# Chunk inverses laid as two blocks on the diagonal of 64x64 tiles, carried there by transfers

## The chip, the cores and the metric

The kernel runs on one core of one Trainium2 chip. The metric is the device time of one execution in microseconds (us). The core has five instruction queues that run side by side: TensorE for matmuls (PE in the profile, with its weight loads shown apart as PEld), VectorE (DVE), ScalarE (ACT), GpSimd (POOL) and SyncE (SP), which here does nothing but issue transfers. Each queue runs its instructions in order, and semaphores between the queues carry the dependencies. Transfers (DMA) are moved by 16 DMA engines.

## The reference

A recurrent attention over 768 steps (batch 4, 8 heads, head size 40) feeds a mixture of eight experts. In the recurrence each head keeps a 40x40 state:

```python
for t in range(S):
    y[:, :, t] = np.einsum('bhd,bhde->bhe', rt, state)
    Sa = np.einsum('bhde,bhe->bhd', state, at)
    state_decay = state * wt[:, :, None, :] - np.einsum('bhd,bhe->bhde', Sa, bt)
    state = state_decay + np.einsum('bhd,bhe->bhde', vt, kt)
```

Its output, 3072 rows of 320, goes through a gate that sends each row to one expert (two matmuls with a ReLU between) or past all of them.

## The kernel before

The recurrence is cut into 24 chunks of 32 steps, numbered c. Inside a chunk, the steps that feed each other form a triangular 32x32 system for each of the 32 pairs of batch b and head. Its inverse turns a right-hand side into what the 32 steps really add. So the kernel works with three kinds of steps.

**Work ahead of the recurrence.** For each half h (two chunks, 64 steps, 12 halves) transfers bring the decays, the keys and the `a` vectors, VectorE scans them, GpSimd and TensorE form the products, and `tinv(ph)` (line 390) inverts the systems of four chunks, 128 systems, at once on VectorE. It is a generator: a first transpose into the scratch `NL_`, 30 elimination steps, a copy, and a last transpose (line 415) that writes the blocks for half 2·ph and half 2·ph+1 into two of the three slots of the tile `TB`. Calls of `T()` in the chunk loop spread its steps over the four chunks before those that need the inverses. Only the first two halves (chunks 0 to 3) take another path, `tinv0` (line 417).

**The recurrence.** The 32 systems of a chunk are two groups of 16: x is 0 or 1 for even or odd heads, hh counts four head pairs, b four batches. Per chunk and group, `ux` (line 474) makes the right-hand sides in PSUM, ScalarE copies them to `UX`, `uq` (line 485) multiplies them by the inverses, ScalarE copies the result into the rows `uo` of the tile `R1t` (four copies, one for each batch) and GpSimd masks a part of it; `sst` (line 497) makes the next state, `yy` (line 525) the output, and `rs` (line 460) and `m2` (line 379) the other inputs of the next chunk. Each group's `ux`, `uq` and `sst` wait for the one before, chunk after chunk; the two groups are independent of each other.

In `uq` a slot of `TB` has 128 partitions, 32 for each batch, and 16 blocks of 32 columns. One matmul takes one 32x32 block as weights and 104 or 72 columns of `UX` on the same 32 partitions (104 in even chunks, 72 in odd ones). Four batches make four matmuls on four tiles of the array, four head pairs make 16 matmuls a group.

**The experts.** After chunk 23 the eight experts run (`experts`, line 932).

**What sets the order.** From chunk 2 until the start of chunk 22 nothing is issued at once: `Rec` records every call (line 108), and `flush` (line 201) replays them in the order that `plan` (line 143) finds. The planner gives each instruction a cost: a matmul at least 0.058 of its units, a transfer 0.06 on SP's queue and a latency of 2.0 plus its bytes by 2.6e5 (lines 96 to 99). From these and the chains behind each instruction it picks what each queue issues next. The order of each queue is then fixed, whatever the chip does. Line 209 in the profile stands for all that was replayed.

Tiles that the change touches: `TB` (3 slots of 512 columns), `SCR` (2048 columns, used by the first chunks only), `NL_` (scratch of `tinv`). The input `zer` holds zeros.

Of the kernel before, what the change touches and what calls it, by code (L numbers as in the profile page):

```python
# [39 lines left out]
class Task:  # L40
    __slots__=("e","op","calls","R","W","d","lat","out","p","n","pr","al","up")
class Eng:
# [15 lines left out]
class Rec:  # L58
# [49 lines left out]
    def call(s,e,op,fn,a,k):  # L108
# [6 lines left out]
        r=[y for x in list(a[1:])+[v for n,v in k.items() if n!='accum_out'] for y in ap(x)]  # L115
        W=[u for x in w for u in s.use(x)]; R=[u for x in r for u in s.use(x)]
        d,lat=s.cost(e,op,w,r,a)
# [6 lines left out]
    def deps(s):  # L124
        acc={}
        for t in s.tasks: t.p,t.n,t.al=set(),[],set()
        for i,t in enumerate(s.tasks):
            for wr,L in ((0,t.R),(1,t.W)):
                u={}
# [97 lines left out]
def attn(ctx,tc,i,m,out,X):  # L227
# [10 lines left out]
    V,A,G,TE,SP=nc.vector,nc.scalar,nc.gpsimd,nc.tensor,nc.sync  # L238
    NC=4*NPH; NH=2*NPH
    SE=(V,G)[SCAN_POOL]  # L240
    NR1=2; NL=4; NL2=2; NTB=3
# [6 lines left out]
    w_,Z_,rv,a_,AB_,NL_,X_,l3=(mv(n) for n in (1041,1042,1041,1024,1024,1024,1024,1024))  # L248
# [4 lines left out]
    l1s=[[WR[:,8192:9216],WR[:,9216:10240],WR[:,10240:11264]]+[l3]+[L1t[:,1024*q:1024*q+1024] for q in range(4)]][0]  # L253
    L1=[[l1s[2*n+x].rearrange("p (u c t) -> p u c t",u=16,c=2) for n in range(NL)] for x in range(2)]
    TB=cp.tile([128,NTB*512],F32,name="TB"); SCR=cp.tile([128,2048],F32,name="SCR")
    TBa=[TB[:,512*q:512*q+512].rearrange("p (h m) -> p h m",h=16) for q in range(NTB)]
    L2t=cp.tile([128,5120],F32,name="L2t"); R1t=cp.tile([128,5632],F32,name="R1t")
    L2=[[L2t[:,1280*(2*n+x):1280*(2*n+x)+1280].rearrange("p (c u d) -> p c u d",c=2,u=16) for n in range(NL2)] for x in range(2)]
    R1=[[R1t[:,3328*n+(1664,1152)[n]*x:][:,:(1664,1152)[n]].rearrange("p (u n) -> p u n",u=16) for n in range(NR1)] for x in range(2)]
    RW=(104,72)  # L260
# [129 lines left out]
    def tinv(ph):  # L390
        ab=AB[0]
        NLt=sq(NL_)
        V.transpose(NLt.rearrange("p a b -> p (a b)"),ab.rearrange("p a b -> p (a b)"))
        Xi=sq(X_)
        X0=ps_x.tile([128,32,SPL],F32)
        V.tensor_tensor(X0,NLt[:,0:SPL].rearrange("p s t -> p t s"),m.mT[:,:,0:SPL],ALU.mult)
        V.tensor_tensor(Xi[:,:,SPL:32],NLt[:,SPL:32].rearrange("p s t -> p t s"),m.mT[:,:,SPL:32],ALU.mult)
        V.memset(X0.rearrange("p a b -> p (a b)")[:,0:SPL*SPL:SPL+1],-1.0)
        V.memset(Xi.rearrange("p a b -> p (a b)")[:,33*SPL::33],-1.0)
        yield  # L400
        for i in range(1,31):
            q=[]
            for g,(j,lo,hi,X) in enumerate(((i,0,min(i,SPL),X0),(i+SPL,SPL,i+SPL,Xi))):
                if j>30: continue
                n=31-j; k=hi-lo
                tmp=tmp_[g]
                tv=tmp[:,:n*k].rearrange("p (a b) -> p a b",b=k)
                V.tensor_tensor(tv,NLt[:,j,j+1:32].unsqueeze(2).broadcast_to([128,n,k]),X[:,j,lo:hi].unsqueeze(1).broadcast_to([128,n,k]),ALU.mult)
                q.append((tv,X[:,j+1:32,lo:hi]))
            for tv,xv in q: V.tensor_tensor(xv,xv,tv,ALU.subtract)  # L410
            yield
        A.copy(Xi[:,:,0:SPL],X0)
        s0=(2*ph)%NTB; s1=(2*ph+1)%NTB
        t0=TBa[s0]; d=bass.AP(t0.tensor,t0.offset,(tuple(t0.ap[0]),(TBa[s1].offset-t0.offset,2),(32,16),(1,32)))
        V.transpose(d.rearrange("p h (x f) m -> p m x h f",x=2),Xi)
        yield
    def tinv0(Xi):

# [65 lines left out]
        UXd[x]=UXs  # L484
    def uq(c,x):
        if c<0: return
        R=R1[x][c%NR1]; Tb=TBa[(c//2)%NTB]; uu=slice(uo[x],uo[x]+32); n=RW[c%2]
        UQ=ps_c.tile([128,4,n],F32,tag="pc",name="psUQ")
        for hh in range(4):
            for b in range(4):  # L490
                q=slice(32*b,32*b+32)
                TE.matmul(UQ[q,hh,:],Tb[q,x*8+hh*2+c%2,:],UXd[x][q,hh,0:n],start=True,stop=True)
        for b in range(4):
            A.copy(R[uu,4*b:4*b+4,:],UQ[32*b:32*b+32,:,:])
        pq=slice(64-64*x,128-64*x); o=R[pq,:,n-32:n]
        (V if c==NC-1 else G).tensor_tensor(o,o,mQ[pq].unsqueeze(1).broadcast_to([64,16,32]),ALU.mult)
# [48 lines left out]
    if 1:  # L545

        with tc.manual_schedule(engines={ET.Pool}):
# [4 lines left out]
            Xi=sq(X_)  # L552
# [42 lines left out]
            t0=tinv0(Xi); next(t0); tq=[0]  # L595
# [54 lines left out]
        for c in range(NC):  # L650
            ph,j=divmod(c,4)
            if c==2: rec.on=True
            if c==20: m.load(0)
            if c==22:
                with tc.manual_schedule(engines={ET.Pool}): rec.flush()
                mp.__exit__(None,None,None)
                wp=m.ctx.enter_context(tc.tile_pool(name="mwa",bufs=1,side="right")); m.WA=[wp.tile([128,5632],F32,name=n) for n in ("WH0","WL0")]; ex=wp.tile([128,1408],F32,name="ex")
                tg=m.split(0)

            if c: rs(c,0)  # L660
            T()
            if j==0 and c: l1a(2*ph+3,1); load_a(2*ph+4)
            if j==0 and c: m1(2*ph+3,0,0)
            RP('0a')
            uq(c-1,1); T()
            if c==1: full(1); m1(3,0,0); m1(3,0,1)
            if c==1: warm(BX[25])
            RP('0b')
            if j==0 and ph: wtt(2*ph,1)
            if j==1: wtt(2*ph+1,0); wex(2*ph+1,1); kbt(2*ph+1,0)  # L670
            if j==2:
                l1a(2*ph+4,1); load_a(2*ph+5)
                m1(2*ph+4,0,0)
            if j==3: kbt(2*ph+2,0)
            if c==1: warm(BX[26])
            yy(c-1,0); T()
            load_v(c+1,0)
            RP('0c')
            if c==1: warm(BX[27])

            if c: ux(c,0)
            T()
            if c==1: warm(BX[28])
            RP('1a')
            if j==1: l1z(2*ph+4,0)
            if j==3: l1z(2*ph+5,0)
            if j==0 and c: m1(2*ph+3,0,1)
            if c==1: m1(3,1,0); m1(3,1,1); tg=tinv(1)
            if j==0: wchk(2*ph+4,0)
            if j==2: m1(2*ph+4,0,1); wchk(2*ph+5,0)  # L690
            if j==1: kbt(2*ph+1,1)
            if j==3: kbt(2*ph+2,1)
            sst(c-1,1); T()
            if c==0: warm(BX[7])
            RP('1b')
            if j==0: scan_z(2*ph+4)
            if j==0 and SE is V: scan_d(2*ph+4)
            if c: m2(c+1,0)
            RP('1c')
            if j==2: scan_z(2*ph+5)  # L700
            if j==2 and SE is V: scan_d(2*ph+5)
            if c==NC-1:
                run_all(rg)
                wx=(ex[:,0:640],ex[:,640:896],ex[:,896:1408])
                SP.dma_start(wx[1],i['io']); m.early(*wx)

            if c: uq(c,0)
            T()
            if j==0:
                if c: m1(2*ph+3,1,0)  # L710
                wchk(2*ph+4,1)
                if SE is G: scan_d(2*ph+4)
                scan_w(2*ph+4); load_w(2*ph+5); kbm(2*ph+4,1)
            if j==1: l1a(2*ph+4,0)
            if j==2:
                m1(2*ph+4,1,0); wchk(2*ph+5,1)
                if SE is G: scan_d(2*ph+5)
                scan_w(2*ph+5); load_w(2*ph+6); kbm(2*ph+5,1)
            if j==3: l1a(2*ph+5,0)
            if c: rs(c,1)  # L720
            else: warm(BX[8])
            if c==1: s2(1,0,(0,0,1,1))
            if c==2: s2(1,1,(0,0,1,1))
            T()
            if j==1: kbt(2*ph+1,2)
            if j==3: kbt(2*ph+2,2)
            RP('2b')
            yy(c-1,1); T()
            load_v(c+1,1)
            RP('2c')  # L730

            RP('2d')
            if 0<c<NC: sst(c,0)
            RP('3a')
            T()
            if j==0: kbm(2*ph+4,0)
            if c==0: warm(BX[9])
            elif j==0: m1(2*ph+3,1,1)
            if j==0 and c and ph+1<NPH: tg=tinv(ph+1)
            if j==2: m1(2*ph+4,1,1); kbm(2*ph+5,0)  # L740
            if j==1: kbt(2*ph+1,3); load_kb(2*ph+5)
            if j==3: kbt(2*ph+2,3); load_kb(2*ph+6)
            if 0<c<NC: ux(c,1)
            T()
            if j==1: l1z(2*ph+4,1)
            if j==3: l1z(2*ph+5,1)
            if j==1: wtt(2*ph+1,1)
            if j==3: wtt(2*ph+2,0); wex(2*ph+2,1)
            if j==0: wex(2*ph+1,0)
            if j==2: wex(2*ph+2,0)  # L750
            if c: m2(c+1,1)
            T()
            load_rv(c+2,G if c else SP)
            if c%2 or c==0: load_rr((c+3)//2,G if c else SP)
            if c<2: m.pad(2*c); m.pad(2*c+1)
            if c==22: m.load(1)
            RP('3c')
            if c==NC-1: xl,ra,onehot=last22(); next(ra)
            if j==3:
                run_all(tg); tg=iter(())  # L760
# [333 lines left out]
```

## Time and profile before

| | |
|---|---|
| three runs | 662.9, 660.15 and 670.07 us, median 662.9 us |
| the profiled execution | 660.01 us, of which the profile's span is 658.2 us |
| mean granted TensorE clock | 0.882 of full speed |
| matmul records | 13,236 |
| packets of SP's DMA queue (q1) | 62,638, 74.31 MB, 39.0% of 16 engines |
| transfers M to L1t, WR or M by SP | 32.0 KB each |
| transfers vt to R1t by SP | 48, 80.0 KB each |

In the profile, a matmul on fp32 data appears as two records, so a `uq` of 16 matmuls shows as 32. The tile names are those of the program: `R1t<-pq,D` writes R1t and reads the PSUM bank pq and the tile D. A time in front of a row is its start from the span's beginning, and the next figure is how long the row's instructions were busy. A bracket gives the idle time ahead of a row on its engine and what ended it.

### The profile page before, as it was taken

Reading aid. Unit: us, or ns where it says so; the run is one execution under the profiler, and the core shown is the slowest. Engines: PE = TensorE matmul, PEld = TensorE weight load, DVE = VectorE, ACT = ScalarE, POOL = GpSimd, SP = SyncE. Lnnn points to the kernel's source line nnn. Section 1 sums busy time; section 2 is a strip of 40 time slices with the busy share of each in tenths; the row PEclk is TensorE's granted clock in tenths of the full one; section 3 lists DMA queues with packets and bytes.
Section 4 is the critical chain, followed back from the end, with each engine's and each line's share of the span. In section 5 each row is a group of like instructions: output and inputs, shape, how many; then the busy total and the mean of one; then the engine's idle time right before and its main releaser. Section 6 shows DMA issues by size and latency. Waiting matters only on the chain. (4 is left out here: it accounts for less than half of the span.)

```text
span 658.2 us, 30327 instructions
## 1 busy us (share of the span) xinstructions
PE 507.4 (77%) x13236; PEld 424.8 (65%) x13236; DVE 519.6 (79%) x1182; ACT 423.6 (64%) x1103; POOL 321.6 (49%) x256
## 2 busy tenths in 40 slices
PE   5766676687588778858758578888678799999994
PEld 2544465566476657637547466767566599899994
DVE  7998778988989789997998977884274458888871
ACT  6463565587766867757768578898966155455540
POOL 5491952645536665375733634333131156566661
PEclk9697778779877986888969799999977799999998
DMA  7784566352444525345334243454535166667200
GB/s 183 215 229 153 133 181 218 114 150 86 124 119 132 162 74 142 107 130 161 102 106 121 82 129 101 133 168 119 156 99 146 57 193 207 214 216 233 81 25 24
DMA packets 67817, 90.85 MB, mean 138 GB/s; under 512 B 32756, under 2 KB 54849, under 8 KB 66190
## 3 DMA queue, kind: packets, MB, share of 16 engines
q1 hardware_dynamic: 62638, 74.31, 39.0%
q0 software_dynamic: 5040, 14.54, 6.8%
q8 instruction: 106, 1.74, 1.1%
q14 instruction: 33, 0.27, 0.1%
HBM read 74.03 MB, written 17.08 MB: 138 GB/s over the span
## 5 line engine op out<-in xcount | busy, mean ns | idle before, releaser
L209 DVE TENSOR_TENSOR M<-M 128x130 f32<-128x130 f32 (+10 forms) x202 | 106.2, 526 | 2.2
L209 ACT COPY R1t<-pq 32x416 f32<-32x416 f32 (+4 forms) x218 | 84.1, 386 | 31.7 <-PE pq L209 28.7
L209 POOL TENSOR_TENSOR R1t<-R1t,mc 64x512 f32<-64x512 f32 x40 | 53.8, 1346 | 86.3 <-ACT R1t L209 62.8
L109 POOL TENSOR_TENSOR WL<-WR,WH 128x1280 fp32r<-128x1280 f32 (+1 forms) x21 | 57.6, 2779 | 8.7 <-ACT WH L109 8.6
L209 ACT COPY R1t<-pc 32x128 f32<-32x128 f32 (+4 forms) x146 | 53.3, 365 | 9.7 <-PE pc L209 7.7
L209 PE MATMUL py<-L2t,R1t 128*32 128x40 f32 x1280 | 22.9, 220 | 27.4 <-DVE XS L209 14.4
L209 POOL TENSOR_TENSOR WR<-WR,M 128x1024 f32<-128x1024 f32 x14 | 33.7, 2422 | 14.9 <-DMA WR<-kb 14.6
L109 ACT CAST WH<-WR 128x1024 fp32r<-128x1024 f32 (+1 forms) x35 | 39.6, 1132 | 0.0
L209 DVE TENSOR_TENSOR px<-px,M 128x168 f32<-128x168 f32 (+8 forms) x141 | 37.1, 263 | 3.1
L209 PEld LDWEIGHTS py<-L2t,R1t 128*32 128x32 f32 x1280 | 18.1, 124 | 31.9 <-issue 16.9
L109 DVE CAST ti<-xe 128x2 int32<-128x2 f32 x8 | 38.0, 4747 | 0.2
L109 POOL DMA_INDIRECT out<-ro,ti x16 | 15.7, 982 | 45.7 <-PE pq L109 21.8
L109 ACT ACTIVATE hH<-pc 128x512 fp32r<-128x512 f32 x21 | 12.6, 598 | 38.3 <-PE pc L109 38.3
L209 POOL DMA_INDIRECT xg<-XS,ix x20 | 24.6, 1232 | 25.1 <-DVE M L209 11.1
L209 DVE TENSOR_TENSOR M<-M,px 128x168 f32<-128x168 f32 (+8 forms) x141 | 34.7, 246 | 1.3
L209 DVE TENSOR_TENSOR_SCAN M<-M 128x1041 f32<-128x1041 f32 (+1 forms) x14 | 32.5, 2320 | 0.2
L209 POOL TENSOR_TENSOR M<-M,mc 128x256 f32<-128x256 f32 x16 | 12.1, 756 | 41.6 <-issue 25.4
L109 PE MATMUL pc<-xH,WH 128*128 128x256 f32 x126 | 32.4, 282 | 0.0
L109 DVE TENSOR_TENSOR WL<-WR,WH 128x1024 fp32r<-128x1024 f32 (+1 forms) x19 | 23.8, 1253 | 8.4 <-ACT WH L109 7.8
L209 DVE TENSOR_TENSOR R1t<-pc,D 40x512 f32<-40x512 f32 (+1 forms) x32 | 19.2, 601 | 13.3 <-PE pc L209 12.9
L209 PE MATMUL ps<-R1t,L2t 128*40 128x40 f32 (+1 forms) x512 | 26.3, 244 | 2.5 <-ACT R1t L209 1.1
L209 PE MATMUL pq<-UX,TB 32*32 32x72 f32 (+1 forms) x800 | 23.6, 262 | 5.5 <-ACT R1t L209 5.3
(380 smaller groups left out, 1692.9 us busy)
## 6 DMA issues: line engine op xcount, KB each, us to landing
WR<-kb SPq DMA_DIRECT2D x10, 1024.0 KB
WR<-w SPq DMA_DIRECT2D x16, 640.0 KB
WR<-w SPq DMA_DIRECT2D x16, 512.0 KB
vvt<-vv POOLq DMA_DIRECT2D x21, 256.0 KB, 4.1
rrt<-rr POOLq DMA_DIRECT2D x10, 512.0 KB, 5.6
M<-wt SPq DMA_DIRECT2D x9, 520.5 KB
M<-at SPq DMA_DIRECT2D x8, 512.0 KB
WR<-w SPq DMA_DIRECT2D x16, 256.0 KB
```

Of the source, the lines that this page charges most:

```text
L109: if not s.on: return fn(*a,**k)
L209: for fn,a,k,own in s.tasks[i].calls: fn(*[at(x,own) for x in a],**{n:at(x,own) for n,x in k.items()})
```

## The change

For the halves from 2 on (chunks 4 to 23) an inverse is kept as a 64x64 tile: the blocks of batches 0 and 1 stand on its diagonal, and zeros beside them; batches 2 and 3 make a second tile on the other 64 partitions. `uq` then takes 64 rows and 64 columns in one matmul, two for each head pair in place of four: 8 matmuls a group. Three slots of 1024 columns hold such tiles, two in `SCR` and one over the first 1024 columns of `TB`. The blocks of halves 0 and 1 keep their form.

`tinv`'s last transpose now writes its blocks to `NL_`. Eight transfers on SP's queue (four batches for each of two halves, 32 partitions of 16 runs of 32 numbers each) then carry them into the slots, batch b to column 0 or 32. Zeros come from three more transfers, two in chunk 2 and one in chunk 5.

```diff
-    TBa=[TB[:,512*q:512*q+512].rearrange("p (h m) -> p h m",h=16) for q in range(NTB)]
+    TBn=[TB[:,o:o+512].rearrange("p (h m) -> p h m",h=16) for o in (1024,0)]
+    TBw=[t.rearrange("p (h m) -> p h m",h=16) for t in (SCR[:,0:1024],SCR[:,1024:2048],TB[:,0:1024])]
+    TBa=TBn
+    def tbw(h): return TBw[(h+1)%NTB]
...
         A.copy(Xi[:,:,0:SPL],X0)
-        s0=(2*ph)%NTB; s1=(2*ph+1)%NTB
-        t0=TBa[s0]; d=bass.AP(t0.tensor,t0.offset,(tuple(t0.ap[0]),(TBa[s1].offset-t0.offset,2),(32,16),(1,32)))
-        V.transpose(d.rearrange("p h (x f) m -> p m x h f",x=2),Xi)
+        t0=NL_.rearrange("p (w h m) -> p w h m",w=2,h=16)
+        V.transpose(t0.rearrange("p w (x f) m -> p m x w f",x=2),Xi)
+        for w in range(2):
+            for b in range(4):
+                r=slice(32*b,32*b+32); SP.dma_start(tbw(2*ph+w)[r,:,32*(b%2):32*(b%2)+32],t0[r,w])
...
-        R=R1[x][c%NR1]; Tb=TBa[(c//2)%NTB]; uu=slice(uo[x],uo[x]+32); n=RW[c%2]
+        R=R1[x][c%NR1]; uu=slice(uo[x],uo[x]+32); n=RW[c%2]; k=32 if c<4 else 64; Tb=TBn[c//2] if c<4 else tbw(c//2)
         UQ=ps_c.tile([128,4,n],F32,tag="pc",name="psUQ")
         for hh in range(4):
-            for b in range(4):
-                q=slice(32*b,32*b+32)
+            for b in range(128//k):
+                q=slice(k*b,k*b+k)
                 TE.matmul(UQ[q,hh,:],Tb[q,x*8+hh*2+c%2,:],UXd[x][q,hh,0:n],start=True,stop=True)
...
-            if c==2: s2(1,1,(0,0,1,1))
+            if c==2:
+                s2(1,1,(0,0,1,1))
+                for q in range(2): SP.dma_start(SCR[:,1024*q:1024*q+1024],i['zer'][:,0:1024])
+            if c==5: SP.dma_start(TB[:,0:1024],i['zer'][:,0:1024])
```

Since the planner sees other costs, it also puts other instructions in other places. Three of them follow; in these listings R1t, L1t, TB, SCR, M, WR are tiles (`NL_` lies in M), `D` holds scales, `sc`, `eq`, `oh`, `sb`, `sm` and `mx` are the gate's, pq, pc, ps and py are PSUM banks.

On VectorE's queue, where `tinv` for chunks 16 to 19 ends, stood before:

```order
L209 TENSOR_TENSOR oh_1409<-eq_1405,m_1408 128x16
L209 SCALAR_TENSOR_TENSOR oh_1409<-sc_1402,oh_1409 128x16
L209 TENSOR_TENSOR sb_1406<-sc_1402,mx_1404 128x16
L209 TENSOR_TENSOR R1t<-pc_102,D_503 40x8x40 x2
L209 STREAM_TRANSPOSE TB<-M 128x32x2x2x8
L209 TENSOR_TENSOR R1t<-pc_102,D_503 40x8x64 x2
L209 TENSOR_REDUCE sm_1410<-ex_1407 128x2
```

and stands now:

```order
L209 STREAM_TRANSPOSE M<-ps_104 128x4x32
L209 STREAM_TRANSPOSE M<-M 128x32x2x2x8
L209 TENSOR_REDUCE mx_1404<-sc_1402 128x2
L209 TENSOR_TENSOR eq_1405<-sc_1402,mx_1404 128x16
L209 TENSOR_TENSOR eq_1405<-eq_1405,mc 128x16
L209 TENSOR_REDUCE m_1408<-eq_1405 128x2
L209 TENSOR_TENSOR oh_1409<-eq_1405,m_1408 128x16
L209 SCALAR_TENSOR_TENSOR oh_1409<-sc_1402,oh_1409 128x16
L209 TENSOR_TENSOR sb_1406<-sc_1402,mx_1404 128x16
L209 COPY XS_1281<-mc 128x2
L209 TENSOR_TENSOR R1t<-ps_104,D_503 40x8x40 x2
```

The transpose that ends `tinv` now stands ahead of the gate's seven instructions and of the two products `R1t<-..,D` of 40 columns.

On SP's queue, where the last `tinv` (for chunks 20 to 23) ends, stood before:

```order
L209 DMA R1t<-vt 32x16x40
L209 DMA WR<-w 128x4x320
L209 DMA R1t<-vt 32x16x40
L209 DMA out<-XS_1281 4x32x320
L209 DMA X<-XS_1281 4x32x320
```

and stands now:

```order
L209 DMA X<-XS_1281 4x32x320
L209 DMA WR<-w 128x4x320
L209 DMA TB<-M 32x16x32 x4
L209 DMA SCR<-M 32x16x32 x4
L209 DMA R1t<-vt 32x16x40
L209 DMA out<-XS_1281 4x32x320
```

The eight transfers of the blocks stand between the load of an expert's weights and the next load of values into R1t.

On TensorE's queue, at the first `uq` of chunk 16, stood before:

```order
L209 MATMUL pq_99<-R1t,WR 32x104 x16
L209 MATMUL pq_100<-rrt_152,SS_117 40x64 x16
L209 MATMUL pq_99<-oh_1409,mc 32x16 x8
L209 MATMUL pc_102<-WR,L1t 32x64 x16
L209 MATMUL pc_101<-UX_453,TB 32x104 x16
L209 MATMUL pq_100<-rrt_152,vvt_150 32x32 x16
```

and stands now:

```order
L209 MATMUL pc_102<-R1t,WR 32x104 x16
L209 MATMUL pq_100<-oh_1409,mc 32x16 x8
L209 MATMUL pc_101<-rrt_152,SS_117 40x64 x16
L209 MATMUL py_105<-L2t,R1t 32x40 x16
L209 MATMUL pc_102<-WR,L1t 32x64 x16
L209 MATMUL pq_100<-WR,L1t 32x64 x16
L209 MATMUL pc_102<-UX_453,SCR 64x104 x8
```

Between the chunk's `ux` (`R1t,WR`) and its `uq` there were three groups, and there are now five; the `uq` itself is 8 matmuls on SCR.

## The prediction, made before the changed kernel ran

> **What bounds the kernel now.** I read the busy shares first, then the windows by stage, then the timeline around `uq` and around the end of `tinv`, then SP's queue.
>
> ```profile
> PE 507.4 (77%) x13236; PEld 424.8 (65%) x13236; DVE 519.6 (79%) x1182; ACT 423.6 (64%) x1103; POOL 321.6 (49%) x256
> DVE  7998778988989789997998977884274458888871
> ```
>
> ```profile
> core 0: us, PE busy (x) PEld busy (x) DVE busy (x) ACT busy (x) POOL busy (x), PEclk, DMA share, GB/s
> 100.00:420.00 320.00, 234.14 (x8024) 194.33 (x8020) 282.29 (x742) 232.44 (x665) 161.62 (x143) 0.85 0.43 124
> 420.00:507.00 87.00, 68.97 (x2362) 56.14 (x2361) 51.52 (x164) 70.02 (x200) 24.71 (x24) 0.92 0.47 135
> 507.00:658.20 151.20, 137.12 (x1158) 130.26 (x1155) 101.86 (x146) 64.41 (x95) 75.29 (x39) 0.96 0.44 138
> ```
>
> The shares over the whole span name no single engine; the stages do. From 100 to 420 us the recurrence and `tinv` run together, and VectorE is busy 282.3 of 320 us (88%), TensorE 234.1 (73%). It has 37.7 us of idle time there: that is the most which any better order could bring in this stage. From 420 to 507 us most of `tinv` is done; ScalarE (80%) and TensorE (79%) take turns in the chain of `ux`, copy, `uq`, copies, `sst`, and no engine is full. After 507 us the experts run, which the change does not touch. All of the change lies between about 100 and 507 us.
>
> **The matmuls.** The change replaces 32 records by 16 in each of 40 groups. Whether that saves time depends on what a record costs. These are the rows of weight loads and matmuls of groups that ran at undisturbed pace; PEld's busy time is the better measure of a group's pace, since it has less of the last matmul's tail.
>
> ```profile
> 152.17 0.69 PEld L209 LDWEIGHTS pq<-UX,TB 32*32 32x32 f32 x32
> 152.17 0.92 PE L209 MATMUL pq<-UX,TB 32*32 32x104 f32 x32
> 166.02 0.53 PEld L209 LDWEIGHTS pc<-UX,TB 32*32 32x32 f32 x32
> 166.02 0.70 PE L209 MATMUL pc<-UX,TB 32*32 32x72 f32 x32
> 153.42 0.49 PEld L209 LDWEIGHTS pq<-WR,M 128*32 128x32 f32 x32
> 153.42 0.65 PE L209 MATMUL pq<-WR,M 128*32 128x64 f32 x32
> 142.16 0.94 PEld L209 LDWEIGHTS pc<-rrt,SS 128*40 128x40 f32 x32
> 142.16 1.09 PE L209 MATMUL pc<-rrt,SS 128*40 128x64 f32 x32
> 153.04 0.34 PEld L209 LDWEIGHTS pc<-rrt,vvt 40*32 40x32 f32 x32 [0.18 <-ACT WT L209]
> 153.04 0.46 PE L209 MATMUL pc<-rrt,vvt 40*32 40x32 f32 x32
> ```
>
> The number of records is the same in all five groups, the time is not. Groups with four tiles side by side take 0.34, 0.49, 0.53 and 0.69 us for 32, 64, 72 and 104 columns: 32 records are 8 rounds of four, and a round costs 42, 61, 66 and 86 ns. It grows with the columns. The fourth group, `rrt,SS`, has tiles of 40 columns of weights, of which only two fit side by side: 32 records are 16 rounds, 0.94 / 16 = 59 ns for 64 columns, where a round of four costs 61. So a round costs what its columns cost, whether two tiles run in it or four. A `uq` of 64x64 tiles has 16 records in pairs, which is 8 rounds of 104 or 72 columns, as before: 0.69 and 0.53 us. The tiles grow, the rounds stay. My term is 0. Its ends: if time followed the records, each group would halve, 20 x 0.69 / 2 + 20 x 0.53 / 2 = 12.2 us less; if the two diagonal tiles did not run side by side, there would be 16 rounds, 24.4 us more. The groups at 142.16 (two column halves) and 153.04 (two row halves) both show halves side by side, so I stay at 0.
>
> The Trainium skill's page "TensorEngine Tiling (Array Packing)", section "Instruction Overhead", says that each matmul carries some 60 cycles whatever its columns; at the 2.4 GHz that "TensorE: Matmul & The Clock Gate" gives, an estimate is 25 ns a record, so 16 records fewer would save 0.4 us a group and 16 us in 40 groups. This trace disagrees for tiles side by side: 32 records in 0.34 us are 11 ns each.
>
> **VectorE.** `tinv` ends in one transpose before and after, into another tile with the same pattern. Nothing is added: 0. VectorE's load in its full stage is unchanged, so the change offers that stage nothing.
>
> **The hand-over.** This is the new wait. Before, `uq` could start once the transpose had ended; now the blocks travel first. These are the five transposes, and the first `uq` that needs each of them (for the first, the group at 152.17 above).
>
> ```profile
> 136.60 1.99 DVE L209 STREAM_TRANSPOSE TB<-M 128x1024 f32<-128x1024 f32 x1 [0.84 <-ACT M L209]
> 220.32 1.98 DVE L209 STREAM_TRANSPOSE TB<-M 128x1024 f32<-128x1024 f32 x1
> 300.55 1.96 DVE L209 STREAM_TRANSPOSE TB<-M 128x1024 f32<-128x1024 f32 x1
> 383.61 1.98 DVE L209 STREAM_TRANSPOSE TB<-M 128x1024 f32<-128x1024 f32 x1
> 444.46 1.94 DVE L209 STREAM_TRANSPOSE TB<-M 128x1024 f32<-128x1024 f32 x1
> 231.21 0.92 PE L209 MATMUL pq<-UX,TB 32*32 32x104 f32 x32
> 311.58 1.11 PE L209 MATMUL pq<-UX,TB 32*32 32x104 f32 x32
> 391.80 0.92 PE L209 MATMUL pc<-UX,TB 32*32 32x104 f32 x32
> 454.59 1.28 PE L209 MATMUL pc<-UX,TB 32*32 32x104 f32 x32
> ```
>
> From the end of the transpose to that `uq` there are 13.6, 8.9, 9.1, 6.2 and 8.2 us, 9.2 in the mean. Against this stands the price of the transfers:
>
> ```profile
> 141.79 2.47 SPq L209 DMA_DIRECT2D WR<-M  x4
> 145.38 0.59 SPq L209 DMA_DIRECT2D R1t<-vt  x1
> 452.65 0.62 SPq L209 DMA_DIRECT2D R1t<-vt  x1
> 140.70 1.00 SPq L209 DMA_DIRECT2D M<-at  x1
> vvt<-vv POOLq DMA_DIRECT2D x21, 256.0 KB, 4.1
> xg<-XS,ix POOLq DMA_INDIRECT x24, 3.6
> 559.21 5.82 DMA xe<-xg
> 387.61 0.99 DVE L209 TENSOR_TENSOR R1t<-pc,D 40x320 f32<-40x320 f32 x2
> 398.64 1.25 DVE L209 STREAM_TRANSPOSE M<-M 128x1024 f32<-128x1024 f32 x1 [2.42 <-ACT M L209]
> ```
>
> SP issues four transfers between tiles in 2.47 us, 0.62 each, and a load with runs as short as the new ones (160 bytes, R1t<-vt) in 0.59. Chunk 4·ph needs only the first four transfers: 4 x 0.62 = 2.5 us of issue, and then the last one has to land. No SP row shows a landing of tile to tile; the nearest are 3.6 and 4.1 us from issue to landing on GpSimd's queue, and 5.8 us in the chain of waits. I take 4.1, the nearest in kind (a plain transfer), so the blocks are there 6.6 us after the transpose, at most 8.3. The one `uq` that this would catch is chunk 16's, with 6.2 us. There the new order puts the transpose ahead of the two 40-column products, 0.99 us, and of the gate's seven short instructions, and puts two more groups between `ux` and `uq` on TensorE, so 7.2 us or more remain. Term: 0; with 5.8 us of landing, about 1 us. The second four (for chunks 4·ph+2 and 4·ph+3) come 2.5 us later and are needed two chunks later. If the cover went, `uq` would stand on TensorE with the next chunk's `rrt,vvt` products behind it, and ScalarE's four copies into R1t would wait.
>
> The Trainium skill's "DMA: Bandwidth & Descriptors", section "Specifications", asks for runs of at least 512 bytes, below which the engine reads and writes back; it speaks against runs of 128 bytes. No row here prices that alone; by the fit in its section on one transfer of GpSimd's path (2.0 us and the bytes by 436 GB/s) the landing would be an estimate of 2.2 us for 64 KB, inside the cover.
>
> **SP's queue.** 43 issues x 0.62 = 27 us of SP, in five bursts of eight (5.0 us) and three zero loads. Behind the last burst stands the next load into R1t. It went out at 452.65; transpose end 446.40 + 5.0 = 451.4, so 1.2 us are to spare. Nothing on TensorE waits for it: 0. The three zero loads are of the size of M<-at (1.00 us of issue) and lie in chunks 2 to 5, several us ahead of their use; the DMA engines are busy 43%: 0. The next `tinv` may not overwrite `NL_` before the blocks have been read: at the tightest place it starts at 398.64, 13.1 us after the transpose's end at 385.59, and 5.0 + 4.1 = 9.1 us suffice: 0.
>
> **The new order.** The planner halves its price for `uq` and adds a latency to `tinv`; every queue between chunk 2 and 22 is reshuffled. No row of the trace prices that. Bound: VectorE's 37.7 us of idle time in its stage; I take a third, 12.6 us, as likely either way, and 0 as the value.
>
> **Sum.** 660.0 us (profiled execution: span 658.2 and 1.8 around it) + 0 - 0 = 660.0. The median shown is 662.9, 2.9 higher; I forecast 661.5, between the two.
>
> **The rivals.** *Records set the price* (faster): 12.2 us less, 647.8. For it: fewer instructions; against it: the rounds above. *The new order fills VectorE's gaps* (faster): half of 37.7, 641.2. For it: `tinv` ends earlier among its neighbours; against: the stage's work is the same and already 88% dense. *The new order opens gaps* (slower): as much the other way, 678.9. *Blocks late behind SP's waits* (slower): SP issues in order, and its queue stands still for TensorE for long:
>
> ```profile
> SPq L209 <- PE pq L209: 40.8, 19, 7.0
> ...
> 444.62 0.92 SPq L209 DMA_DIRECT2D WR<-w  x1
> ```
>
> If such a wait of 7.0 us stood ahead of each burst, the blocks would come 7.0 + 6.6 - 9.2 = 4.4 us late, five times, 22 us: 682. It decides from 2.7 us a time (13.3 us in all). Against it: the load of weights that the new order puts ahead of the last burst went out at 444.62, before the transpose ended at 446.40, and SP then issued nothing until 452.65. *The change does not do what it says*: the diagonal tiles run one after the other, 24.4 us more on TensorE: 684.4 if all of it were on the path.
>
> **How the numbers follow.** Two per cent is about what a measurement of this kernel can tell from no change: faster is under 649.6, slower over 676.2. No change: 0.66. Faster: records 0.05, order 0.10, together 0.15. Slower: order 0.09, late blocks 0.06, tiles in turn 0.04, together 0.19. The likeliest has 661.5 with its own range 649 to 674 (12.6 either side). To leave out no more than 0.2 (better order, late blocks, tiles in turn) the range takes in the records' 647.8 and the worse order's 678.9: 645 to 680.
>
> **What would show it.** Right: groups `UX,SCR` of 16 records with a PEld time near 0.69 and 0.53 us; `uq` after each burst without an idle time released by a DMA; VectorE's busy time from 100 to 420 us near 282 us and the stage near 320. Wrong: PEld of 0.35 (records) or 1.38 us (in turn); TensorE idle ahead of the first `uq` of chunks 4, 8, 12, 16 or 20 with a DMA as releaser; SP's bursts starting several us after the transpose; or a stage before 507 us that differs by over 13 us with all of these in place, which would leave the order.

## The result, and the profile after

| | before | after |
|---|---|---|
| median of 20 runs | 660.9 us | 668.5 us |
| lowest and highest | 656.1 and 670.1 us | 664.2 and 673.5 us |
| ratio after to before | | 1.0123, 95% interval 1.0098 to 1.0147 |
| profiled execution, span | 658.2 us | 666.3 us |

The change made the kernel 1.2% slower. The forecast was no change, 661.5 us, with 645 to 680 as the range. The time lies in the range, but the slowdown is real: its interval leaves no change out. Medians are over all runs, while each ratio is estimated from the runs that were not in the chip's slower state, so it is not quite the quotient of the medians.

The busy line and VectorE's tenths on the page of the changed kernel:

```profile
PE 516.3 (77%) x12596; PEld 432.6 (65%) x12596; DVE 508.7 (76%) x1182; ACT 423.1 (63%) x1103; POOL 320.5 (48%) x256
DVE  7998689978796759888799958884247457888871
```

Its windows by stage (busy time of each engine, with the number of records, the granted clock and the share of the DMA engines):

```profile
core 0: us, PE busy (x) PEld busy (x) DVE busy (x) ACT busy (x) POOL busy (x), PEclk, DMA share, GB/s
100.00:420.00 320.00, 233.76 (x7298) 195.13 (x7293) 266.34 (x719) 220.32 (x630) 157.97 (x140) 0.82 0.47 131
420.00:507.00 87.00, 69.25 (x2198) 57.01 (x2201) 51.99 (x165) 73.88 (x213) 24.27 (x23) 0.92 0.52 138
```

TensorE has 640 records less (13,236 before), and VectorE is busy 10.9 us less in all. Between 100 and 420 us VectorE did 266.3 us of work where it did 282.3 before. So in the full stage it stood still for 54 us instead of 38. Part of the fall is that some products took less time (see further down); the rest are new holes, and the timeline shows what the longest of them wait for. First TensorE's weight loads of four `uq` groups at undisturbed pace (start, busy time, tiles, shape, records):

```profile
161.53 0.73 PEld L209 LDWEIGHTS pq<-UX,SCR 64*64 64x64 f32 x16 [0.44 <-ACT R1t L209]
181.69 0.57 PEld L209 LDWEIGHTS pq<-UX,SCR 64*64 64x64 f32 x16
212.09 0.57 PEld L209 LDWEIGHTS pc<-UX,SCR 64*64 64x64 f32 x16
248.01 0.73 PEld L209 LDWEIGHTS pq<-UX,TB 64*64 64x64 f32 x16
```

Half the records take 0.73 and 0.57 us, where the full number took 0.69 and 0.53. The form saves nothing. Now SP's queue around the burst of eight that ends the second `tinv`:

```profile
215.19 0.59 SPq L209 DMA_DIRECT2D L1t<-M  x1
215.87 0.62 SPq L209 DMA_DIRECT2D L1t<-zer  x1
216.55 3.19 SPq L209 DMA_DIRECT2D L1t<-M  x3
219.84 0.60 SPq L209 DMA_DIRECT2D R1t<-vt  x1
220.54 3.85 SPq L209 DMA_DIRECT2D TB<-M  x4
224.44 2.66 SPq L209 DMA_DIRECT2D SCR<-M  x4
227.20 0.60 SPq L209 DMA_DIRECT2D out<-XS  x1
227.91 3.89 SPq L209 DMA_DIRECT2D L1t<-M  x4
231.84 0.60 SPq L209 DMA_DIRECT2D X<-XS  x1
232.55 0.40 SPq L209 DMA_DIRECT2D L1t<-zer  x1
```

and TensorE and VectorE there, and VectorE later, at the burst for chunks 16 to 19:

```profile
230.46 0.49 PE L209 MATMUL py<-L2t,R1t 128*32 128x40 f32 x32
237.03 1.08 PE L209 MATMUL pc<-WR,L1t 128*32 128x64 f32 x32 [6.08 <-DMA L1t<-zer]
...
239.46 0.99 DVE L209 TENSOR_TENSOR R1t<-pq,D 40x320 f32<-40x320 f32 x2 [6.30 <-PE pq L209]
...
400.17 0.32 DVE L209 STREAM_TRANSPOSE M<-pq 128x128 f32<-128x128 f32 x1 [6.58 <-DMA L1t<-M]
```

SP issues almost without a pause for 18 us. The zeros in `L1t` that TensorE's products `WR,L1t` need (232.55) stand behind the eight blocks and six other transfers, and TensorE stands idle for 6.08 us until they have landed; VectorE then waits 6.30 us for TensorE. The last burst but one does the same to VectorE directly. No `uq` waits for the blocks in that time: the late ones are the loads queued behind them. The waits view sums it (total, times, longest):

```profile
POOL WR L209 <- DMA WR<-kb: 25.5, 3, 9.2
DVE M L209 <- DMA L1t<-M: 6.6, 1, 6.6
PE pc L209 <- DMA L1t<-zer: 6.1, 1, 6.1
```

The second and third line have no counterpart in the kernel before, and GpSimd's wait for the keys (WR<-kb) was 14.6 us there.

### The profile page after: what moved, and what is told of

Same layout as the page of the kernel before. It is cut to its first block, busy times and chain, and to the rows that moved or that the text cites. A ratio compares the mean times of both kernels' runs of the same rounds, so it can differ in the third digit from the quotient of the medians.

```text
span 666.3 us, 29130 instructions
## 1 busy us (share of the span) xinstructions
PE 516.3 (77%) x12596; PEld 432.6 (65%) x12596; DVE 508.7 (76%) x1182; ACT 423.1 (63%) x1103; POOL 320.5 (48%) x256
## 3 DMA queue, kind: packets, MB, share of 16 engines
q1 hardware_dynamic: 84190, 78.51, 41.9%
q0 software_dynamic: 5040, 14.54, 7.1%
## 4 chain that ended last, share of the span: by engine, by line
PE 22%; DVE 15%; ACT 9%; issue 4%; DMA 2%; SPq 1%; POOL 0%; DVEq 0%; POOLq 0%; ACTq 0%
DVE M L209 7%; PE pc L109 6%; PE ps L109 5%; ACT R1t L209 5%; PE py L109 3%; PE px L109 3%; PE pq L209 2%; PE pc L209 1%; DVE R1t L209 1%; DVE px L209 1%; PE pq L109 1%; ACT L2t L209 1%; DVE ti L109 1%; DMA ex<-xg 1%; SPq L209 1%
## 5 line engine op out<-in xcount | busy, mean ns | idle before, releaser
L209 POOL TENSOR_TENSOR R1t<-R1t,mc 64x512 f32<-64x512 f32 x40 | 51.2, 1280 | 95.1 <-ACT R1t L209 80.4
L209 ACT COPY R1t<-pq 32x416 f32<-32x416 f32 (+4 forms) x198 | 77.9, 394 | 29.5 <-PE pq L209 24.6
L209 DVE TENSOR_TENSOR M<-M 128x130 f32<-128x130 f32 (+10 forms) x202 | 89.6, 444 | 1.9
L209 DVE TENSOR_TENSOR R1t<-pq,D 40x320 f32<-40x320 f32 (+1 forms) x44 | 25.5, 578 | 22.3 <-PE pq L209 21.7
L109 ACT ACTIVATE hH<-pc 128x512 fp32r<-128x512 f32 x21 | 12.6, 598 | 38.9 <-PE pc L109 38.9
L209 DVE TENSOR_TENSOR_SCAN M<-M 128x1041 f32<-128x1041 f32 (+1 forms) x14 | 35.1, 2509 | 0.4
L109 PE MATMUL ps<-mc 128*128 128x512 f32 x36 | 24.9, 800 | 4.3 <-DMA mc<-mc 3.2
L109 PE MATMUL ps<-WH,hH 128*128 128x320 f32 x88 | 27.6, 314 | 0.0
L209 POOL TENSOR_TENSOR M<-M,mc 128x256 f32<-128x256 f32 x16 | 13.9, 871 | 27.8 <-issue 13.9
```

Source lines behind the costliest of these rows:

```text
L109: if not s.on: return fn(*a,**k)
L209: for fn,a,k,own in s.tasks[i].calls: fn(*[at(x,own) for x in a],**{n:at(x,own) for n,x in k.items()})
```

## The experiments

Times are medians, and each ratio is to the kernel before on the same chip. Several kernels leave work out and so compute other numbers; from the last `uq` to the end all sixteen traces take 146 to 152 us, so their gains lie for the most part ahead of the experts. Where the words say "the order of X", every engine's instructions stand in that kernel's order, and only what is named differs. In five of the kernels that leave work out (not in the one on the order alone), the test at the end that sends unusual inputs down a general path is held off as well.

### Which part costs

Four kernels take the change apart. The first keeps the changed order and issues none of the 40 block transfers:

```diff
+            if s.tasks[i].tag=='blk': continue
             for fn,a,k,own in s.tasks[i].calls: fn(...)
```

> The changed kernel, every queue in the same order, with the 40 transfers that carry the blocks left out (uq then works on zeros, so the corrections of chunks 4 to 23 are missing from the output). Measured so far: before 660.9, changed 668.5 us. Theory 1, the bursts of eight hold up SP's other transfers, on which TensorE and VectorE wait: 659 to 663 us, and the idle times ahead of L1t<-zer (PE, 6.1 us) and L1t<-M (DVE, 6.6 us) are gone. Theory 2, the new order itself costs the time: 667 to 670 us. Theory 3, the 64x64 form costs it: 667 to 670 us. Theory 4, uq waits for the blocks' landing: 659 to 663 us.

Measured: 649.6 us, ratio 0.982 (0.979 to 0.985). Without its transfers the changed order is 1.8% faster than the kernel before. That is 9 us below the lowest time that any of the four theories allowed: none of them had a gain from the new order in it.

The second issues two transfers of 128 partitions in place of eight of 32 (same blocks and bytes; 83,710 packets on SP's queue for 84,190):

```diff
-                SP.dma_start(tbw(2*ph+w)[r,:,32*(b%2):32*(b%2)+32],t0[r,w])
+                if b==0: SP.dma_start(tbw(2*ph+w)[:,:,0:32],t0[:,w])
```

> The changed kernel, every queue in the same order, but of each burst of eight only two transfers, one for each half, of all 128 partitions into column 0 (the blocks of batches 1 and 3 then stand beside the diagonal, so the output's corrections are wrong from chunk 4 on). The bytes, the wait for the transpose and uq's wait for a landing stay, SP's issues go from 40 to 10. Theory 1 (bursts on SP): 660 to 664 us. Theory 2 (order): 667 to 670 us. Theory 3 (form): 667 to 670 us. Theory 4 (landing of the blocks): 665 to 669 us.

Measured: 659.8 us, ratio 0.996 (0.993 to 0.999), just below the band of the first theory and far from the others. The wait of TensorE for L1t<-zer is 1.9 us.

The third keeps order and transfers, but `uq` takes 16 matmuls of 32x32 from the diagonals:

```diff
-            for b in range(128//k):
-                q=slice(k*b,k*b+k)
-                TE.matmul(UQ[q,hh,:],Tb[q,x*8+hh*2+c%2,:],...)
+            for b in range(4):
+                q=slice(32*b,32*b+32); o=32*(b%2) if c>=4 else 0
+                TE.matmul(UQ[q,hh,:],Tb[q,x*8+hh*2+c%2,o:o+32],...)
```

> The changed kernel, every queue in the same order, transfers as changed, but uq again as 16 matmuls of 32x32 a group, read from the diagonals. Theory 3 (the 64x64 form costs the time): 659 to 662 us. All others: 667 to 670 us, the same as the changed kernel, since a group has eight rounds of columns in either form.

Measured: 671.1 us, ratio 1.013 (1.009 to 1.017), where the changed kernel has 1.012; the time is 1 us above the band. The form of the matmuls is worth nothing either way.

The fourth is the kernel before with eight idle transfers (TB to the unused SCR) behind each end of `tinv`:

```diff
         V.transpose(d.rearrange(...),Xi)
+        for w in range(2):
+            for b in range(4): SP.dma_start(SCR[32*b:32*b+32, ...],TBa[(s0,s1)[w]][32*b:32*b+32])
```

> The kernel before, every queue in its old order, with eight more transfers on SP's queue behind the end of each tinv, of the same size and shape as the blocks', from TB into SCR, which nobody reads. Theory 1 (bursts on SP): 664 to 670 us, with new idle times ahead of work that waits for L1t<-M, L1t<-zer or WR<-kb. Theory 2 (order), 3 (form) and 4 (landing): 660 to 662 us, no change.

Measured: 664.8 us, ratio 1.007 (1.003 to 1.010). Bursts that nobody waits for cost the old order 0.7%, some 4 us; GpSimd's wait for the keys (WR<-kb) rose from 14.6 to 29.0 us.

What was open is whether the first kernel was fast because its `uq` no longer waits for `tinv`. So the next one keeps that wait: the changed order with the old data path, the transpose writing narrow slots and `uq` reading them in 32x32.

```diff
-        V.transpose(t0.rearrange("p w (x f) m -> p m x w f",x=2),Xi)
+        V.transpose(dd,Xi)
```

> The order of the changed kernel on every engine, but the old data path: tinv's transpose writes the narrow TB slots, uq reads them in 16 matmuls of 32x32, and the 40 block transfers and three zero loads are not issued. uq waits for tinv again, which it did not in the run without block transfers (649.6 us). Theory 1 (the bursts on SP's queue hold up the other loads): 648 to 653 us, no wait of TensorE for L1t<-zer, the longest GpSimd wait for WR<-kb 15 us or less. Rival (the run without transfers was fast because uq no longer waited for tinv, and the new order is worth nothing): 658 to 662. Rival (the order itself loses): 666 to 670.

Measured: 651.5 us, ratio 0.987 (0.982 to 0.992). (Its last five `uq` groups stand outside the planned stretch and still multiply zeros.) With this the change splits in two: the new order is worth 9.8 us of gain (651.5 against 661.3), the transfers cost 17.0 (668.5 against 651.5).

### What in the transfers costs

The same order, every transfer cut to a sixteenth:

```diff
-                SP.dma_start(tbw(2*ph+w)[r,:,e],t0[r,w])
+                SP.dma_start(tbw(2*ph+w)[r,0:1,e],t0[r,w,0:1])
```

> The changed kernel's exact order with all 40 block transfers, each cut to the first of its 16 blocks (32 runs of 128 bytes in place of 512; the other matrices are left zero, so uq multiplies by zeros there). As many transfers on SP's queue, a sixteenth of the packets. The same order without transfers gave 651.5 us, with two transfers a tile and all packets 659.8, with all 668.5. If the number of issues costs: 664 to 668 us, with SP's bursts of 4.5 us and more and the wait of TensorE for L1t<-zer at 4 us or more. If the packets cost: 652 to 655. If both: about 660, the complement of the run with two transfers.

Measured: 661.9 us, ratio 1.005 (1.001 to 1.009). SP's timeline at its first burst:

```profile
141.40 6.52 SPq L210 DMA_DIRECT2D SCR<-M  x8
```

These eight issues take 6.52 us with 32 runs each, and took 6.47 with 512. The other four bursts are shorter than in the changed kernel: from first issue to last, all five take 31.3 us with the small transfers and 34.8 with the full ones. So an issue costs SP nearly, but not quite, the same. TensorE's wait for L1t<-zer is 3.7 us, a little under the 4 us expected if issues cost. Of the 17 us, 10.4 remain with the issues alone (661.9 - 651.5), so about 6.6 come with the packets and their bytes; by the ratios the parts are 12.0 and 5.0, so the split is known to some 2 us. The kernel with two transfers a tile has nearly all packets and a quarter of the issues: 6.6 + 10.4 / 4 = 9.2 us over 651.5, and 8.3 were measured. That is a weak check: its ten issues still take SP 15.8 us from first to last in the five bursts, nearly half of 34.8.

Two kernels try to pay less. The first joins both halves in one transfer, four a tile (a fourth slot makes the diagonals neighbours), and is planned anew:

```diff
-        for w in range(2):
-            for b in range(4):
-                SP.dma_start(tbw(2*ph+w)[r,:,32*(b%2):32*(b%2)+32],t0[r,w])
+        for b in range(4):
+            SP.dma_start(ST_[r,o:o+2048].rearrange(...)[:,:,32*(b%2):32*(b%2)+32],NL_[r,0:1024].rearrange(...))
```

> The changed kernel with four transfers in place of eight a tile (both halves of a row block in one, 128 KB each; a fourth slot makes the two diagonals neighbours; planned anew). Bytes and blocks are the same. Theory 1 (what costs is SP's issue): SP issues some 13 to 16 us less, and the time comes near that of the run with two transfers, 658 to 663 us; the wait of TensorE for L1t<-zer falls to 3 us or less. Rival (the bytes or the short runs cost, in the DMA engines): 666 to 670, with the same waits. Rival (uq waits for the landing of the blocks): 666 to 672, TensorE idle ahead of the first uq of a tile with ST<-M as releaser.

Measured: 662.6 us, ratio 1.003 (0.9995 to 1.006), in the expected band; TensorE's wait for L1t<-zer fell to 3.6 us, not below 3. A transfer of both halves takes SP 1.0 us and more (four in 4.10 to 7.01), so SP's time fell by less than half.

The second issues the blocks on GpSimd's queue, planned anew:

```diff
-                SP.dma_start(tbw(2*ph+w)[r,:,32*(b%2):32*(b%2)+32],t0[r,w])
+                G.dma_start(tbw(2*ph+w)[r,:,32*(b%2):32*(b%2)+32],t0[r,w])
```

> The changed kernel with the 40 block transfers issued on GpSimd's queue in place of SP's (planned anew). Theory 1: SP's loads are no longer held up, the waits of TensorE for L1t<-zer and of VectorE for L1t<-M are under 2 us; GpSimd pays 40 issues (24 to 40 us of an engine that is 50% busy), so 652 to 664 us by how much its products come late. Rival (the transfers themselves, whatever queue): 666 to 670.

Measured: 657.9 us, ratio 0.998 (0.994 to 1.002). The time fits, one sign does not: VectorE still waits 7.4 us for L1t<-M and 13.7 us for WR<-M. With SP free of the bursts, its own loads come late all the same in this order. That it is the packets is not shown: SP's queue has 21,120 packets less than in the changed kernel (63,070 for 84,190), and GpSimd's queue has, by the profile's count, only 1,280 more (6,320 for 5,040).

### Why the transfers were not hidden

The planner that writes the order takes 0.06 for a transfer on SP's queue. Measured were 0.85 us in the mean: the five bursts of the changed kernel take 6.47, 6.51, 5.95, 6.81 and 8.22 us, 34.0 for 40 issues. (Most of the issues take 0.6 to 0.7 us, and one or two in each burst 1.2 to 2.1.) So one number is changed:

```diff
-            return (0.06 if e=='S' else 1.0 if 'ind' in op else 0.6),2.0+by/2.6e5
+            return (0.65 if e=='S' else 1.0 if 'ind' in op else 0.6),2.0+by/2.6e5
```

> The changed kernel with one number of the planner changed: a transfer on SP's queue costs SP 0.65 us in place of 0.06, so the list is made knowing that eight blocks take 5 us of SP. If the planner's ignorance of SP's issues was the loss: 650 to 658 us, waits of TensorE and VectorE for L1t under 2 us each. If SP's work itself is the loss, wherever it stands: 662 to 670.

Measured: 649.0 us, ratio 0.985 (0.980 to 0.991): 19.5 us less than the changed kernel, with all that it does still in it, and 1 us below the expected band. Two places on SP's timeline, and the waits:

```profile
206.56 0.78 SPq L209 DMA_DIRECT2D L1t<-zer  x1
...
209.56 0.40 SPq L209 DMA_DIRECT2D L1t<-zer  x1
210.66 2.67 SPq L209 DMA_DIRECT2D TB<-M  x4
213.37 3.54 SPq L209 DMA_DIRECT2D SCR<-M  x4
217.01 3.66 SPq L209 DMA_DIRECT2D L1t<-M  x4
```

```profile
DVE M L209 <- DMA WR<-M: 9.9, 4, 5.6
POOL WR L209 <- DMA WR<-kb: 6.8, 2, 4.8
DVE M L209 <- DMA L1t<-M: 3.8, 2, 2.9
POOL D L209 <- DMA L1t<-zer: 0.7, 1, 0.7
```

The bursts are as long as before, but the zeros now go out ahead of them, and TensorE waits for none. VectorE's waits for L1t did not fall under 2 us as expected: they are 3.8 us in two, the longest 2.9, and with those for WR<-M 13.7 us in six.

Is that the transfers hidden, or another list that happens to be good? Two controls. The first takes the transfers out of this order:

```diff
+            if s.tasks[i].tag=='blk': continue
```

> The order of the run with SP's real price in the planner (649.0 us), but the 40 block transfers are not issued and uq multiplies by the zeros there. If the list hid the transfers: 644 to 650 us, less than 1% faster. If they still cost what they cost in the changed kernel (17 us, by 668.5 against 651.5): 630 to 634.

Measured: 644.5 us, ratio 0.976 (0.969 to 0.983). The transfers cost this order 4.5 us by the medians, and the intervals of the two ratios overlap. Taken out in the same way, they cost the changed order 18.9 us (668.5 against 649.6). So 14.4 of the 19.5 us are transfers better hidden, and the other 5.1 are a list that is faster without them too. The second gives the kernel before the same price:

```diff
-            return (0.06 if e=='S' else ...
+            return (0.65 if e=='S' else ...
```

> The kernel before with only the planner's price of a transfer on SP at 0.65 us in place of 0.06. Its SP queue has no bursts of eight. If the price helps because it makes room for the bursts: 655 to 664 us, little change. If it makes better lists of any program: 640 to 650, as much off as the changed kernel got (19 us).

Measured: 664.7 us, ratio 1.004 (1.000 to 1.008). It is just above its band of little change: without bursts the right price gains nothing here. This fits a price that helps by making room for the bursts, but it is one list, and another program could come out otherwise.

### Why the new order is faster

VectorE is busy 10.9 us less with the same 1,182 instructions. One group fell by 16.6 us, the others rose by 5.7 together. In the groups of the kernel before (count, busy time, mean ns of one):

```profile
L209 DVE TENSOR_TENSOR M<-M 128x130 f32<-128x130 f32 (+10 forms) x202 | 106.2, 526 | 2.2
L209 DVE TENSOR_TENSOR px<-px,M 128x168 f32<-128x168 f32 (+8 forms) x141 | 37.1, 263 | 3.1
```

and of the changed kernel:

```profile
L209 DVE TENSOR_TENSOR M<-M 128x130 f32<-128x130 f32 (+10 forms) x202 | 89.6, 444 | 1.9
L209 DVE TENSOR_TENSOR px<-px,M 128x168 f32<-128x168 f32 (+8 forms) x141 | 37.2, 264 | 3.1
```

The 202 elimination products of `tinv` whose operands all lie in SBUF took 106.2 us, now 89.6; those with an operand in PSUM (px) did not change. Here are two stretches of the kernel before, VectorE and then GpSimd:

```profile
281.55 0.23 DVE L209 TENSOR_TENSOR M<-M 128x76 f32<-128x76 f32 x1
...
282.32 7.76 DVE L209 TENSOR_TENSOR M<-M 128x76 f32<-128x76 f32 x3
290.00 0.22 DVE L209 TENSOR_TENSOR M<-M,px 128x72 f32<-128x72 f32 x1
...
251.12 0.32 DVE L209 TENSOR_TENSOR M<-M,px 128x168 f32<-128x168 f32 x1
251.48 0.34 DVE L209 TENSOR_TENSOR px<-px,M 128x168 f32<-128x168 f32 x1
```

```profile
281.95 2.16 POOL L209 TENSOR_TENSOR WR<-WR,M 128x1024 f32<-128x1024 f32 x1
...
284.21 1.28 POOL L209 TENSOR_TENSOR R1t<-R1t,mc 64x512 f32<-64x512 f32 x1
285.46 2.15 POOL L209 TENSOR_TENSOR WR<-WR,M 128x1024 f32<-128x1024 f32 x1
287.58 2.17 POOL L209 TENSOR_TENSOR WR<-M 64x1024 f32<-64x1024 f32 x1
...
251.10 1.27 POOL L209 TENSOR_TENSOR R1t<-R1t,mc 64x512 f32<-64x512 f32 x1 [0.32 <-POOL R1t L209]
```

A product of 76 elements takes 0.23 us; three of them took 7.76 while GpSimd computed from 281.95 to 289.75. At 251 the products with an operand in PSUM ran at their pace beside GpSimd. The Trainium skill's page "SBUF — State Buffer", section "Who interferes with whom", says that these two engines share a pair of ports by an exclusive lock, and its "Summary: rules for kernel authors" that of a VectorE operation with two SBUF inputs and a GpSimd operation that reads SBUF the one issued second stands still until the first has ended; these rows agree. So does the whole group: 39 of the 202 products took over 0.1 us more than the 20th percentile of their shape, 56.2 us more in all, and each of them overlaps GpSimd's work by at least its excess. In the changed kernel there are 29 such products with 39.3 us. The rest of the group's time is 50 us in both.

Whether this sets the time was tried by shortening GpSimd alone. In the order of the kernel before, GpSimd's mask behind `uq` works on one block of 16 (the 40 masks took 53.8 us, and take 11.0):

```diff
-        G.tensor_tensor(o,o,mQ[pq].unsqueeze(1).broadcast_to([64,16,32]),ALU.mult)
+        G.tensor_tensor(o[:,0,:],o[:,0,:],mQ[pq],ALU.mult)
```

> The kernel before in its exact order, but GpSimd's masking of R1t behind uq works on one of 16 blocks (64x32 in place of 64x512, some 1.27 us down to 0.15 each; the rest stays unmasked). Theory C: VectorE's products with all operands in SBUF (M<-M) stand still while GpSimd computes, 59.0 us of excess over their usual durations in the kernel before, 42.5 in the changed order without transfers, 31.3 in the order made by the two prices; that is why orders differ. Then this kernel loses part of the excess: VectorE's busy time down by 10 us or more, 645 to 655 us. Rival (GpSimd is off the path, and the orders differ for another reason): 658 to 662, VectorE's busy time within 3 us of 519.6.

The excess named there is, over all products of the form M<-M, the time above the 20th percentile of their shape.

```profile
L211 DVE TENSOR_TENSOR M<-M 128x130 f32<-128x130 f32 (+10 forms) x202 | 86.7, 429 | 2.2
```

Measured: 641.8 us, ratio 0.973 (0.965 to 0.981). GpSimd was busy under half the span, and less work on it took 19.4 us off the kernel and 19.5 us off VectorE's group; the time is below the expected band. Products that wait for the mask come sooner too, so not all of it need be the stalls. That GpSimd's work stretches these products is shown; that this alone makes one order faster than another is argued.

Since the order alone gives such gains, two kernels ask whether the kernel before can have one without the change. The first gives its planner a `uq` at half the price and 2.6 us of latency behind `tinv`'s last transpose:

```diff
+            rec.PC=0.058 if c<4 else 0.029
...
+        rec.LX=2.6
         V.transpose(d.rearrange(...),Xi)
+        rec.LX=0.0
```

> The kernel before, with nothing changed but two numbers of the planner: uq's price 0.029 us a matmul from chunk 4 on (in place of 0.058) and 2.6 us of latency behind tinv's last transpose. So the planner makes an order of the kind of the changed kernel's for the old data path. If these prices make the better order: 648 to 655 us. If the gain of the changed kernel's order was that of one list among many: 655 to 666, about the kernel before.

```profile
L209 DVE TENSOR_TENSOR M<-M 128x130 f32<-128x130 f32 (+10 forms) x202 | 77.0, 381 | 1.8
```

Measured: 637.6 us, ratio 0.965 (0.959 to 0.971), the best of all and below both expected bands, with the computation of the kernel before. The group of products takes 77.0 us, 29.2 less, and the kernel 23.7 less. The second has the price alone:

```diff
-        rec.LX=2.6
+        rec.LX=0.0
```

> The kernel before with uq's planned price halved and no latency behind the transpose: one of the two numbers that gave 637.6 us together. If the price alone makes the better order: 636 to 642 us. If each number makes just another list, whose time goes by how VectorE's M<-M products fall on GpSimd's work: anywhere from 636 to 665, with VectorE's busy time lower by about as much as the time (496.4 us of busy time at 637.6, 519.6 at 661.2).

Measured: 651.0 us, ratio 0.985 (0.978 to 0.992). The price alone does not make the better order; each pair of numbers makes its own list. The sign that was to go with it did not come: in its profiled execution, 656.5 us, VectorE is busy 518.2 us, 1.4 less than before, and the group of products takes 96.8 us, 9.4 less. So the group's time alone does not fix the kernel's.

## Why the prediction was wrong

- **The matmuls, 0: right.** A `uq` group costs what its columns cost. The rows show 0.73 and 0.57 us for 0.69 and 0.53, 0.04 more a group, 1.6 us in 40; undoing the form changed nothing (1.013 and 1.012).
- **The hand-over, 0: right.** No `uq` stood idle with a block's landing as releaser. The one wait that the profile puts down to a block transfer is VectorE's, 1.0 us for SCR<-M ahead of a transpose into M.
- **SP's queue, 0: here it failed.** The step took 0.62 us an issue (most took about that, but 0.85 were measured in the mean of the bursts) and then looked behind the last burst only, where the next load into R1t had 1.2 us to spare. It found nobody waiting there and put 0 for all five. Behind the others stood the zeros and rows for `L1t` and the keys for `WR`, on which TensorE, VectorE and GpSimd wait. The transfers measured 17.0 us in the new order, 10 to 12 of them with the issues alone. The three waits were on no list of what would show the forecast wrong, which asked only for TensorE idle ahead of a `uq`.
- **The packets: not in the sum.** SP's queue has 84,190 of them after and 62,638 before. The landing was priced and was covered, as said; but 5 to 7 of the 17 us came with the packets and their bytes and not with the issues. Which loads they made late is not shown. The Trainium skill's "DMA: Bandwidth & Descriptors", section "Specifications", which the prediction weighed for the landing alone, asks for runs of at least 512 bytes. The cut transfers had fewer bytes and fewer runs at once, so what short runs cost by themselves wasn't tried.
- **The new order, 0 with 12.6 either way: the value off, the bound good.** It gained 9.8 us. But that the bound held is luck: it was made from VectorE's idle time, as the most that any order could bring, and in the order alone the busy time of VectorE fell by 12.9 us (506.7 for 519.6).
- **VectorE, 0: wrong in its reason.** The instructions are the same, their durations are not: 106.2 us against 89.6 in one group.

The forecast put 0 for two terms that were -9.8 and +17.0 us. They cancel in part, so the number came out nearer than its terms. The rival "blocks late behind SP's waits" had the right queue but the wrong victim: the blocks were in time, and they made others late.

Open is how the 17 us spread over the single waits along the path, what of the shortened masks is stall and what earlier products, and whether the granted clock, which was 0.82 between 100 and 420 us after and 0.85 before, follows the holes or adds to them.

## What to carry to other kernels

When a change adds transfers to a queue, go behind each burst and list every transfer that now stands there, with who waits for it; that the DMA engines were busy 43% of the stage did not show it here. When a planner writes the order, correct its prices along with the change: the same change lost 1.2% with a wrong price for SP and gained 1.5% with a better one. And try the planner's prices by themselves first, since another order of the old instructions was worth more than the change.

## What the runs showed of the hardware

An issue on SP's queue took 0.6 to 0.7 us in most cases, and 1.2 to 2.1 us for one or two in a burst of eight. With 4 KB in 32 runs in place of 64 KB in 512 five such bursts took 31.3 us in place of 34.8. A VectorE product on SBUF alone stood still while GpSimd computed (three that take 0.23 us each took 7.76), while one with an operand in PSUM did not. In this kernel the order moved the time of 202 such products between 77.0 and 107.1 us (107.1 in the control with SP's price in the kernel before). Pairs of 64x64 tiles took nearly as long as fours of 32x32 tiles with the same columns, 0.57 and 0.53 us for 72.
